# Moving the load targets of a decode kernel from 128 bytes behind a multiple of 512 in SBUF to the multiple itself

## The chip, the cores and the metric

The kernel runs on one core of one Trainium2 chip. The metric is the device time of one execution in microseconds (us). TensorE is called PE below, its loading of weights PEld, VectorE DVE, ScalarE ACT, GpSimd POOL and SyncE SP. SBUF is the memory on the chip in which tiles lie: 128 partitions, and within each partition a tile occupies a run of bytes that starts at the same address in all of them. DMA engines, 16 of them for a core, copy from the main memory (HBM) into these runs. A DMA is cut into packets; here a packet is the run of one partition, for example 32768 bytes.

## What is computed

One decoding step for two sequences: normalised input, attention over the last 4096 entries of a cache with 8 key and value heads, and beside it a dense layer with the Mish activation. The results are added to the input.

```python
def _A_ref(x, k_cache, v_cache, wq, wo):          # x: (2, 1, 448); caches: (2, 8, 32768, 256), bf16
    W = 4096
    q = (x @ wq).reshape(2, 1, 16, 256).transpose(0, 2, 1, 3)
    k = jnp.repeat(k_cache[:, :, Sk - W:, :], 2, axis=1)
    v = jnp.repeat(v_cache[:, :, Sk - W:, :], 2, axis=1)
    scores = jnp.einsum("bhqd,bhkd->bhqk", q, k) * (256 ** -0.5)
    p = softmax(scores)
    o = jnp.einsum("bhqk,bhkd->bhqd", p, v)
    return o.transpose(0, 2, 1, 3).reshape(2, 1, 4096) @ wo      # wo: (4096, 448)

def _B_ref(x, w1, b1, w2):                         # w1: (448, 1792), w2: (1792, 448)
    h = x @ w1 + b1
    return (h * jnp.tanh(softplus(h))) @ w2

xn = layernorm(A_x)
out = A_x + _A_ref(xn, ...) + _B_ref(xn, ...)
```

All of the 4096 keys and values of 16 heads (2 sequences by 8 heads) are read once: 2 x 16 x 4096 x 256 x 2 bytes = 67.1 MB, and some 10 MB of weights.

## The kernel before

Tiles come out of pools. A pool takes its bytes in SBUF in the order in which pools are opened, right behind the pool before it:

```python
    k_pool = ctx.enter_context(tc.tile_pool(name="kk", bufs=2))     # 2 x 32768 bytes per partition
    v_pool = ctx.enter_context(tc.tile_pool(name="vv", bufs=3))     # 3 x 16384
    kt_pool = ctx.enter_context(tc.tile_pool(name="kt", bufs=1))    # 2 x 32768
    wo_pool = ctx.enter_context(tc.tile_pool(name="wo", bufs=2))    # 2 x 7168
    p_pool = ctx.enter_context(tc.tile_pool(name="pp", bufs=1))
    consts = ctx.enter_context(tc.tile_pool(name="consts", bufs=1))
    small = ctx.enter_context(tc.tile_pool(name="small", bufs=2))
```

In front of the first pool lie 16384 bytes that the framework keeps and four constants of its own in 128 bytes. So the first tile of keys starts at 16512 = 32 x 512 + 128.

The loads are all issued by SP, in one queue:

```python
    def load_k(u, r):                 # 4 MB: 128 packets of 32768 bytes
        t = k_pool.tile([P, RK * KE], BF16, tag="k", name="k")
        src = kview[u][:, s0:, :].rearrange("j (c t) d -> c j (t d)", c=C)
        nc.sync.dma_start(out=t[:], in_=src[:, :, r * RK * KE : (r + 1) * RK * KE])

    def load_v(u, g, lo=0, hi=T):     # 2 MB: 128 packets of 16384 bytes
        ...
        nc.sync.dma_start(
            out=t[:, lo * Dh : hi * Dh], in_=src[g, :, :, lo * Dh : hi * Dh]
        )
    # ... load_wo: rows of 7168 bytes, for the last round of 1792; wq: 16384 and 12288; w1: 12544

    w2_parts = ((0, 0, NI), (1, 0, 4), (1, 4, 6), (1, 6, NI))      # NI = 7

    def load_w2(part):                # into a tile of the key pool, in four pieces
        if part == 0:
            state["w2"] = k_pool.tile([P, RK * KE], BF16, tag="k", name="w2")
        k, lo, hi = w2_parts[part]
        w2_in = B_w2.flatten().rearrange("(k p e) -> k p e", k=2, p=P)
        at = k * NI * D               # D = 448, two bytes each
        nc.sync.dma_start(
            out=state["w2"][:, at + lo * D : at + hi * D],
            in_=w2_in[k, :, lo * D : hi * D],
        )
```

The work runs in four rounds u; each round's keys are turned by DVE, scored by PE, and its values weighed by PE:

```python
    for u in range(U - 1):
        load_k(u + 1, 0); load_v(u, 0); load_v(u, 1)
        load_k(u + 1, 1); load_v(u, 2); load_v(u, 3)
        load_wo(u)
        turns(u + 1, 0)               # DVE: kt <- k, 128x4096 fp32 each
        values(u, 0); values(u, 1)    # PE: pv += p' v
        scores(u + 1, 0)              # PE: sc <- kt, qd; ACT: exp; DVE: p <- ex
        ...
    # last round: values, then the output projection and the second dense product
    for part in range(len(w2_parts)):
        dense_out(part)               # PE: acc += act' w2
    ...
    nc.sync.dma_start(out=out.flatten_outer_dims(), in_=res[:])
```

Of the kernel before, what the change touches and what calls it, by code (L numbers as in the profile page):

```python
# [11 lines left out]
BF16 = mybir.dt.bfloat16  # L12
# [5 lines left out]
def kernel(  # L18
# [14 lines left out]
    P = 128  # L33
# [5 lines left out]
    Bsz, Sq, D = A_x.shape  # L39
# [20 lines left out]
    NI = F2 // P  # L60
# [4 lines left out]

    ctx.enter_context(tc.manual_schedule())

    k_pool = ctx.enter_context(tc.tile_pool(name="kk", bufs=2))
    v_pool = ctx.enter_context(tc.tile_pool(name="vv", bufs=3))
    kt_pool = ctx.enter_context(tc.tile_pool(name="kt", bufs=1))  # L70
# [119 lines left out]
    for x in range(2):  # L190
        for w in range(4):
            at = 32 * w + (2 * (w % 2) + x) * NQ
# [52 lines left out]
    def add_rows(lhsT, rows, stop=False):  # L245
        for g in range(G):
            nc.tensor.matmul(  # L247
                acc[32 * g : 32 * g + Bsz, :],
                lhsT=lhsT,
                rhs=rows[:, g * DG : (g + 1) * DG],  # L250
                start=False,
                stop=stop,
                skip_group_check=True,
            )
# [257 lines left out]
    def mish():  # L512
# [20 lines left out]
        nc.vector.tensor_tensor(out=t_sb[:], in0=t_sb[:], in1=den[:], op=ALU.mult)  # L533
        nc.vector.tensor_tensor(out=act_bf[:], in0=h_sb[:], in1=t_sb[:], op=ALU.mult)

    w2_parts = ((0, 0, NI), (1, 0, 4), (1, 4, 6), (1, 6, NI))

    def load_w2(part):
        if part == 0:
            state["w2"] = k_pool.tile([P, RK * KE], BF16, tag="k", name="w2")  # L540
        k, lo, hi = w2_parts[part]
        w2_in = B_w2.flatten().rearrange("(k p e) -> k p e", k=2, p=P)
        at = k * NI * D
        nc.sync.dma_start(
            out=state["w2"][:, at + lo * D : at + hi * D],
            in_=w2_in[k, :, lo * D : hi * D],
        )

    def dense_out(part):
        k, lo, hi = w2_parts[part]  # L550
        for i in range(lo, hi):
            at = (k * NI + i) * D
            add_rows(
                act_bf[:, i, k, :], state["w2"][:, at : at + D], stop=(k == 1 and i == NI - 1)
            )
# [39 lines left out]
    for part in range(len(w2_parts)):  # L595
        load_w2(part)
# [12 lines left out]
    for part in range(len(w2_parts)):  # L609
        dense_out(part)  # L610
# [40 lines left out]
```

## Time and profile before

| | before |
|---|---|
| median of 3 executions | 191.78 us (191.65 to 191.96) |
| span of the profiled execution | 189.5 us |
| busy: PE, DVE, ACT | 93.9, 89.2, 12.3 us |
| read from HBM | 77.67 MB, 410 GB/s over the span |
| key load, 4096 KB, issue to landing | 30.3 us, median of 8 |
| value load, 2048 KB, issue to landing | 27.3 us, median of 15 |

The span is the time from the first to the last instruction in the trace. The busy times of engines run beside each other and don't add up to it. "Issue to landing" includes the time that a load stands in the queue behind older loads. In the row of 40 slices each digit is the busy share of a fortieth of the span, in tenths, 9 standing for 90% and more. The chain of work that ended last is followed backwards from the last instruction, each step to what released it.

### The profile page before, as it was taken

What the parts mean: (1) busy time and instruction counts of PE and PEld (TensorE: products, weight loads), DVE (VectorE), ACT (ScalarE), POOL (GpSimd) and SP (SyncE); (2) the same over time, 40 slices, a digit from 0 to 9 for tenths busy, and PEclk for the clock granted to TensorE, in tenths of its full rate; (3) what the DMA queues carried; (4) which work ended last, traced back from release to release, by engine and by line L of the source; (5) the groups of instructions that cost most, each with busy time, mean ns of one, the idle gap of its engine ahead of it and who ended that gap; (6) DMA issues with size and microseconds to landing.
All of it is one profiled execution on the core that took longest, in us unless ns stands there. A gap on an engine that the chain in (4) does not pass through costs nothing.

```text
span 189.5 us, 1989 instructions
## 1 busy us (share of the span) xinstructions
PE 93.9 (50%) x873; PEld 38.0 (20%) x873; DVE 89.2 (47%) x81; ACT 12.3 (7%) x23; POOL 4.0 (2%) x16
## 2 busy tenths in 40 slices
PE   0301545565139103869248033868475044969673
PEld 0100121521012001423112011413121011513361
DVE  6629643974980097017930394029900691040001
ACT  3000031001000100110001000110001001010201
POOL 8000000000000000000000000000000000000000
PEclk9999999755555855576855755555557655555975
DMA  6999999999999999999999999999999999999990
GB/s 222 443 388 425 468 408 408 456 439 401 425 495 422 387 410 436 432 429 432 429 456 429 398 429 465 423 398 418 432 456 432 398 420 431 432 406 430 404 377 28
DMA packets 5871, 77.78 MB, mean 410 GB/s; under 512 B 868, under 2 KB 1640, under 8 KB 2408
## 3 DMA queue, kind: packets, MB, share of 16 engines
q1 hardware_dynamic: 5588, 77.66, 96.7%
q8 instruction: 6, 0.10, 0.2%
q10 hardware_dynamic: 276, 0.01, 0.1%
q14 instruction: 1, 0.01, 0.0%
HBM read 77.67 MB, written 0.00 MB: 410 GB/s over the span
## 4 chain that ended last, share of the span: by engine, by line
DMA 81%; PE 9%; DVE 3%; issue 3%; SPq 2%; ACT 1%; DVEq 0%
DMA v<-in_A_v_cache_dram 59%; DMA k<-in_A_k_cache_dram 15%; DMA w<-in_B_w_dram 7%; PE pv L390 5%; DVE kt L267 2%; PE sc L345 2%; PE o L410 1%; PE acc L247 1%; PE dn L368 1%; SPq L103 1%; SPq L132 1%; SPq L95 1%; DVE p L356 0%; ACT ex L353 0%; ACT vs L404 0%
## 5 line engine op out<-in xcount | busy, mean ns | idle before, releaser
L267 DVE STREAM_TRANSPOSE kt<-k 128x4096 f32<-128x4096 f32 x16 | 70.1, 4417 | 41.0 <-DMA k<-in_A_k_cache_dram 41.0
L390 PE MATMUL pv<-v,p 128*32 128x512 bf16 x240 | 26.2, 583 | 53.7 <-DMA v<-in_A_v_cache_dram 53.7
L345 PE MATMUL sc<-kt,qd 128*32 128x512 bf16 x256 | 28.2, 614 | 3.2 <-DVE kt L267 1.8
L390 PEld LDWEIGHTS <-p 128*32 128x32 bf16 x240 | 8.5, 123 | 71.1 <-issue 64.6
L437 DVE TENSOR_TENSOR oT<-o,rec 128x16 bf16<-128x16 f32 x4 | 0.7, 174 | 29.5 <-PE o L410 16.6
L345 PEld LDWEIGHTS <-qd 128*32 128x32 bf16 x256 | 8.6, 134 | 19.6 <-issue 17.7
L356 DVE STREAM_TRANSPOSE p<-ex 128x512 bf16<-128x512 bf16 x8 | 5.2, 690 | 15.4 <-ACT ex L353 15.4
L472 PE MATMUL early<-wo,ox 128*2 128x448 bf16 x24 | 9.4, 570 | 0.8 <-ACT ox L462 0.8
L353 ACT ACTIVATE ex<-sc 128x512 bf16<-128x512 f32 x8 | 4.8, 597 | 76.5 <-PE sc L345 76.5
L289 PE MATMUL q_ps<-wq,xs 128*32 128x512 bf16 x28 | 3.4, 625 | 11.9 <-DMA wq<-in_A_wq_dram 11.9
L410 PE MATMUL o<-sel,vs 128*128 128x8 f32 x32 | 6.7, 339 | 2.8 <-ACT vs L404 2.8
L410 PEld LDWEIGHTS o<-sel,vs 128*128 128x128 f32 x32 | 6.4, 293 | 6.0 <-ACT vs L404 6.0
L368 PE MATMUL dn<-p,ones 128*128 128x512 bf16 x8 | 4.3, 540 | 6.0 <-DVE p L356 6.0
L404 ACT COPY vs<-pv 128x512 f32<-128x512 f32 x4 | 2.3, 586 | 47.2 <-PE pv L390 47.2
L502 PE MATMUL h_ps<-xs,w 128*128 128x4 bf16 x49 | 2.8, 193 | 4.3 <-DMA w<-in_B_w_dram 4.3
L334 PE MATMUL sc<-mneg,ident 128*128 128x512 bf16 x8 | 4.8, 595 | 0.0
L210 PE MATMUL xr_ps<-ident,xrows 2*128 2x2 bf16 x7 | 1.0, 181 | 6.6 <-DVE xrows L209 6.6
L376 DVE TENSOR_REDUCE rec<-dn 128x8 f32<-128x512 f32 x4 | 2.8, 692 | 2.5 <-PE dn L368 2.5
L289 PEld LDWEIGHTS <-xs 128*32 128x32 bf16 x28 | 1.0, 126 | 13.9 <-issue 13.9
L502 PEld LDWEIGHTS <-w 128*128 128x128 bf16 x49 | 2.7, 152 | 5.2 <-DMA w<-in_B_w_dram 5.2
L472 PEld LDWEIGHTS <-ox 128*2 128x2 bf16 x24 | 2.5, 115 | 5.5 <-issue 4.4
L453 PEld LDWEIGHTS <-hot 128*64 128x64 bf16 x48 | 2.0, 142 | 2.6 <-issue 2.6
(62 smaller groups left out, 37.7 us busy)
## 6 DMA issues: line engine op xcount, KB each, us to landing
k<-in_A_k_cache_dram SPq DMA_DIRECT2D x8, 4096.0 KB, 30.3
v<-in_A_v_cache_dram SPq DMA_DIRECT2D x15, 2048.0 KB, 27.3
wo<-in_A_wo_dram SPq DMA_DIRECT2D x3, 896.0 KB, 24.0
wq<-in_A_wq_dram SPq DMA_DIRECT2D x1, 2048.0 KB, 16.8
w<-in_B_w_dram SPq DMA_DIRECT2D x1, 1568.0 KB, 32.1
wq<-in_A_wq_dram SPq DMA_DIRECT2D x1, 1536.0 KB, 19.8
v<-in_A_v_cache_dram SPq DMA_DIRECT2D x1, 1536.0 KB, 10.0
wo<-in_A_wo_dram SPq DMA_DIRECT2D x2, 448.0 KB, 15.5
```

What stands on the lines that cost most here:

```text
L267: nc.vector.transpose(out=kt[i][:, :, :, r, :], in_=t[:, r * KE : (r + 1) * KE].bitcast(FP32).rearrange("p (a c j) -> p a c j", c=P // (R ...
L289: nc.tensor.matmul(q_ps[32 * u : 32 * (u + 1), :], lhsT=xs[:, s, :], rhs=wq_t[s][:, u * 512 : (u + 1) * 512], start=(s == 0), stop=(s == N ...
L334: nc.tensor.matmul(sc[:].rearrange("p t c m -> p (t c m)"), lhsT=ident[:], rhs=mneg[:].rearrange("p a j -> p (a j)"), start=True, stop=Fal ...
L345: nc.tensor.matmul(sc[32 * w : 32 * (w + 1)].rearrange("p t c m -> p t (c m)"), lhsT=qd[:, u, 2 * n + e, :, :].rearrange("p g q -> p (g q) ...
L353: nc.scalar.activation(out=ex[:, :, :, i, :], in_=sc[:], func=ACT.Exp, scale=scale)
L356: nc.vector.transpose(out=p_t[h][:].rearrange("p g t q -> p t g q"), in_=ex[:, h * TH : (h + 1) * TH].rearrange("p t c i m -> p t (c i m)" ...
L368: nc.tensor.matmul(dn[:].rearrange("p a q -> p (a q)"), lhsT=ones[:], rhs=p_t[i][:].rearrange("p g t q -> p (g t q)"), start=(i == 0), sto ...
L376: nc.vector.tensor_reduce(out=rec[:], in_=dn[:].rearrange("p a q -> p q a"), axis=AXIS.X, op=ALU.add)
L390: nc.tensor.matmul(pv[32 * w : 32 * (w + 1), :, :].rearrange("p x d -> p (x d)"), lhsT=p_t[a // 4][:, g, 4 * (a % 4) : 4 * (a % 4) + 4, :] ...
L410: nc.tensor.matmul(po[:, c, :], lhsT=sb[:, x, c::2], rhs=sel[:, x, :], start=(x == 0 and c == 0), stop=(last and x == 1), skip_group_check ...
L472: nc.tensor.matmul(early[:], lhsT=ox[:, i, :], rhs=w[:, i, :], start=False, stop=(u == U - 2 and i == 7),)
L502: nc.tensor.matmul(h_ps[:, i, :, :].rearrange("p k b -> p (k b)"), lhsT=w1_v[:, s, i, :], rhs=xs[:, s, 0 : 2 * Bsz], start=(s == 0), stop= ...
```

## The change

A tile of 192 bf16 values, 384 bytes per partition, is taken from a pool that is opened first. Nothing writes or reads it. It moves every tile behind it by 384 bytes: 128 + 384 = 512. And the second half of w2 starts 4096 values (8192 bytes) behind the first half in its tile, and not 3136 values (6272 bytes), which is no multiple of 512. The purpose is that the tiles which loads fill begin at multiples of 512 bytes.

```diff
+    lead_pool = ctx.enter_context(tc.tile_pool(name="lead", bufs=1))
+    lead_pool.tile([P, 192], BF16, name="lead")
     k_pool = ctx.enter_context(tc.tile_pool(name="kk", bufs=2))
     v_pool = ctx.enter_context(tc.tile_pool(name="vv", bufs=3))
...
+    KH = 4096
     w2_parts = ((0, 0, NI), (1, 0, 4), (1, 4, 6), (1, 6, NI))
...
-        at = k * NI * D
+        at = k * KH
         nc.sync.dma_start(
             out=state["w2"][:, at + lo * D : at + hi * D],
...
-            at = (k * NI + i) * D
+            at = k * KH + i * D
             add_rows(
                 act_bf[:, i, k, :], state["w2"][:, at : at + D], stop=(k == 1 and i == NI - 1)
```

The addresses in both programs, as built, and what they leave when divided by 512:

| tile | before | rest | after | rest |
|---|---|---|---|---|
| k, first and second buffer | 16512, 49280 | 128 | 16896, 49664 | 0 |
| v (also wq, w1), three buffers | 82048, 98432, 114816 | 128 | 82432, 98816, 115200 | 0 |
| wo, two buffers | 196736, 203904 | 128 | 197120, 204288 | 0 |
| w2, first half | 16512 | 128 | 16896 | 0 |
| w2, second half, pieces 1, 2, 3 | 22784, 26368, 28160 | 256, 256, 0 | 25088, 28672, 30464 | 0, 0, 256 |

## The prediction

> **What bounds the kernel now.** I read the page's DMA rows first, because the time is long against the engines' work: PE is busy for 50% of the span and DVE for 47%.
>
> ```profile
> span 189.5 us, 1989 instructions
> ...
> DMA  6999999999999999999999999999999999999990
> ...
> DMA packets 5871, 77.78 MB, mean 410 GB/s; under 512 B 868, under 2 KB 1640, under 8 KB 2408
> ...
> q1 hardware_dynamic: 5588, 77.66, 96.7%
> ```
>
> The DMA row stands at 9 from the second slice to the last but one, and the packets of the one big queue take 96.7% of the time of 16 DMA engines. So 0.967 x 189.5 = 183.2 us of each DMA engine is packet time. Next I looked at whether the chain of work agrees.
>
> ```profile
> DMA 81%; PE 9%; DVE 3%; issue 3%; SPq 2%; ACT 1%; DVEq 0%
> ```
>
> It does: 81% of what ended last is transfer, and the PE and DVE pieces on it are places where a load's issue waited for a buffer while older loads kept the DMA engines full. The table by stretches shows that such waits leave no hole in the stream (columns: stretch, its us, busy us of PE, PEld, DVE, ACT, POOL, granted clock, DMA share, GB/s):
>
> ```profile
> 12.00:24.00 12.00, 3.37 (x28) 0.99 (x28) 8.77 (x2) 0.54 (x1) 0.00 (x0) 1.00 1.03 437
> 24.00:60.00 36.00, 18.52 (x174) 7.75 (x178) 22.96 (x22) 2.75 (x5) 0.00 (x0) 0.66 0.99 423
> 60.00:100.00 40.00, 19.61 (x160) 7.37 (x156) 19.91 (x9) 1.95 (x4) 0.00 (x0) 0.63 1.01 429
> 100.00:140.00 40.00, 21.40 (x160) 7.96 (x163) 19.78 (x9) 1.95 (x4) 0.00 (x0) 0.54 1.01 430
> 140.00:172.00 32.00, 18.08 (x148) 6.63 (x140) 11.14 (x7) 1.82 (x4) 0.00 (x0) 0.55 1.00 421
> ```
>
> The DMA share is 1.0 in each, at 421 to 437 GB/s. Last, the end of the timeline:
>
> ```profile
> 185.49 0.83 PE L247 MATMUL acc<-w,act_bf 128*2 128x112 bf16 x17 [0.25 <-DMA w<-in_B_w_dram]
> ...
> 187.53 0.33 SPq L620 DMA_DIRECT2D out_dram<-res  x1
> ```
>
> The last weights land just before 185.5 us and what follows is about 4 us of closing work. So the time is: 2.2 us until the first packet starts, 183.2 us of packets, 4.1 us after them (that makes the span, 189.5), and 191.78 - 189.5 = 2.3 us outside the span. The kernel is bound by its own load stream from end to end, and only a shorter packet can shorten it.
>
> **What the Trainium skill says.** First, "DMA: Bandwidth & Descriptors", Specifications: the ceiling of the SBUF side is 435 GB/s, 16 engines by 32 bytes by 850 MHz, which is 27.2 bytes per ns for one engine. The trace agrees: the stretches above lie at 421 to 437 GB/s.
>
> Second, the same page, "How a descriptor splits into AXI transactions": transfers are cut at multiples of 256 bytes, and a start that is no such multiple makes the first transaction begin at the boundary below, which costs beats of 32 bytes for nothing. Before the change nearly all big tiles start 128 bytes past such a boundary: 4 beats, 4 / 0.85 = 4.7 ns per packet, an estimate from this page. The trace agrees only in part, as shown below.
>
> Third, "SBUF — State Buffer", "SBUF: two separate sides": engines and DMA reach SBUF by separate ports and do not disturb each other. So I count no gain from a changed meeting of transfers and engines. The trace neither proves nor contradicts it.
>
> Fourth, the same page, "Operand start alignment": it settles what addresses are legal and says of its own runs that they timed nothing. So no page gives a speed for 128 against 512 bytes, and the number must come from this trace.
>
> **The change, part by part.** It adds no instruction and removes none; the order on every engine is as before with shifted line numbers. The lead tile is never written or read; it costs 384 bytes per partition. All tiles behind it move by 384 bytes, so their places relative to each other stay, except that the second half of w2 lies 8192 bytes behind the first and no longer 6272. Engines should run each operation as before: the DVE transposes of 4403 ns and the matmuls keep their shapes and strides. What is left is the DMA packet.
>
> So I took the packet records of the trace: size and duration of each. What a packet takes beyond its bytes / 27.2 I call its excess:
>
> - 16384 bytes need 602.4 ns. The fastest tenth took 611 ns, the median 615, the slowest tenth 619.
> - 32768 bytes need 1204.7 ns. The same three were 1213, 1218 and 1221 ns.
> - Over all sizes there is a floor of about 8.3 ns of excess, some 7 beats. For most of the kernel packets lie at the floor, 4 to 5 ns above it, or 8 to 9 ns above it.
>
> The sum per DMA engine: 77.66 MB / 16 / 27.2 = 178.5 us for the bytes. The 4994 packets of more than 500 bytes are 312 per engine, and 312 x 8.3 ns = 2.6 us of floor. Ordinary excess above the floor (packets up to 60 ns over their bytes) sums to 1.05 us. Single packets with 60 to 800 ns excess, mostly the first one of each engine, give 0.77 us, and the little semaphore packets 0.34 us. Together 178.5 + 2.6 + 1.05 + 0.77 + 0.34 = 183.2, the packet time from above. The bytes cannot shrink. An address can touch only the 1.05 us above the floor and perhaps the floor itself.
>
> Does the misplacement cause the 1.05 us? The kernel before holds its own controls:
>
> - For: the three last pieces of w2 lie at multiples of 256 already (tile at 16512, plus 6272, 9856 and 11648 bytes: 22784, 26368, 28160). Of their 384 packets 376 are at the floor. In the same last microseconds, of 123 packets of 6272 and 4096 bytes that start 128 behind a boundary, only 84 are.
> - Against: until 23 us all tiles start 128 behind, and yet all 128 packets of 16384 bytes that fall there (the first wq piece) are at the floor, and so are 126 of the 128 packets of 12288 bytes. A fixed fee of 4.7 ns per misplaced start would show there. From 23 us on only 361 of 1920 packets of 16384 bytes are at the floor.
>
> So the fee isn't fixed, and either it arises from misplacement together with something that begins at 23 us, or from that something alone and the w2 pieces were lucky in their hour. I give the first about two chances in five. The expected gain is then 0.4 x 1.05 = 0.42 us, and 191.78 - 0.42 is about 191.4 us.
>
> **The rivals.** (1) Nothing happens: the stream is at the port's rate whatever the address, and the spread of 4 to 9 ns comes from the memory that is read, whose addresses don't change. For it speaks the clean stretch until 23 us. That gives 191.8 us, with the 0.2 us by which the three runs differ.
>
> (2) The whole spread is misplacement: 191.78 - 1.05 = 190.7 us. For it speak the w2 pieces, and that the steps of 4 to 5 ns have the size of the page's 4 beats.
>
> (3) The floor goes too. The fetches of instructions, 8192 bytes each, show 307 ns at their fastest against 301.2 for the bytes, 5.8 ns excess and not 8.3. If a wholly placed packet comes down to that, 312 x 2.5 ns = 0.8 us more, 189.9 us. Against it: the packets of w2 at multiples of 256, the last of them at a multiple of 512, have the same 8.1 to 8.6 ns as misplaced ones.
>
> (4) Slower: some engine reads worse at the new address, or the moved half of w2 meets another tile. All shifts are multiples of 128 bytes, and DVE and PE have slack: half of the span idle. DVE's transposes stand on the chain with 2% of the span, so even a tenth more on each would hardly reach 0.4 us. That gives at most 192.2 us. I see nothing that speaks for it.
>
> **Range and chances.** The centre is 191.4 us. Between rival 2 with a part of rival 3 below and rival 1 with its scatter above, a range of 190.5 to 192.0 should hold it 8 times in 10. A change of 2% is 3.8 us. All that is not bytes sums to 4.8 us and most of it is floor and start, so faster by over 2% gets 0.02, slower by over 2% 0.01, and within 2% the remaining 0.97.
>
> **What the profile after would show.** If rival 2 holds, the median 16384-byte packet falls from 615 to 611 ns and the median 32768-byte one from 1218 to 1213 ns; queue q1's share times the span falls from 183.2 to about 182.2 us, and the last weights land about 1 us earlier. If rival 1 holds, these stay within 1 ns and 0.3 us. If rival 3 holds, the fastest tenth of 16384-byte packets falls below 611 ns. DVE's 4403 ns per transpose and the engines' busy sums should be equal within a per cent in all cases. I would be wrong if DMA shares below 0.98 appeared in the stretches above (a hole in the stream), or if packets gained more than their whole excess, which would mean that 27.2 bytes per ns is not the limit I take it for.

## The result, and the profile after

The changed kernel takes 190.7 us (median of 4, 190.38 to 190.9) against 191.85 us for the kernel before on the same chip (median of 4). The ratio is 0.994 with a 95% interval from 0.9921 to 0.9958: between 0.8 and 1.5 us are gone, about 0.6%. That lies in the stated range and within 2%.

The page of the changed kernel, the lines that answer to those shown of before:

```profile
span 188.2 us, 1989 instructions
...
DMA  6999999999999999999999999999998999999990
...
DMA packets 5871, 77.78 MB, mean 413 GB/s; under 512 B 868, under 2 KB 1640, under 8 KB 2408
...
q1 hardware_dynamic: 5588, 77.66, 96.8%
...
DMA 80%; PE 10%; DVE 3%; issue 3%; SPq 2%; ACT 1%; DVEq 0%
```

The same packets, the same bytes and the same full row of 9s. The queue's share hardly moves, because the span shrank with it: 0.968 x 188.2 = 182.2 us of packets for each DMA engine, where 183.2 us stood before. The chain has the same owner with the same weight. A share says nothing here; share times span does.

The stretches of the changed kernel (stretch, its us, busy us of PE, PEld, DVE, ACT, POOL, granted clock, DMA share, GB/s):

```profile
24.00:60.00 36.00, 18.18 (x178) 7.86 (x182) 22.97 (x22) 2.63 (x4) 0.00 (x0) 0.68 0.99 425
60.00:100.00 40.00, 21.27 (x160) 7.74 (x156) 19.78 (x9) 1.95 (x4) 0.00 (x0) 0.54 1.01 434
100.00:140.00 40.00, 21.19 (x160) 7.75 (x152) 19.78 (x9) 1.95 (x4) 0.00 (x0) 0.54 1.01 434
```

There is no hole before or after: the DMA share is 1.0 in both. (A packet counts whole in the stretch in which it starts, so a short stretch can show a share of 1.03.) But 425, 434 and 434 GB/s pass where 423, 429 and 430 passed. The engines' work is what it was, as DVE's costliest group shows, first before and then after, with means of 4417 and 4414 ns:

```profile
L267 DVE STREAM_TRANSPOSE kt<-k 128x4096 f32<-128x4096 f32 x16 | 70.1, 4417 | 41.0 <-DMA k<-in_A_k_cache_dram 41.0
...
L269 DVE STREAM_TRANSPOSE kt<-k 128x4096 f32<-128x4096 f32 x16 | 70.0, 4414 | 39.9 <-DMA k<-in_A_k_cache_dram 39.9
```

At the end of the timeline everything is 1.3 us earlier, and lengths differ by 0.05 us at most (PE was at 185.49 us when it took the last weights, the output was issued at 187.53):

```profile
184.22 0.78 PE L249 MATMUL acc<-w,act_bf 128*2 128x112 bf16 x17 [0.26 <-DMA w<-in_B_w_dram]
...
186.25 0.33 SPq L623 DMA_DIRECT2D out_dram<-res  x1
```

The packet records show where the time came from. "At the floor" means at most 9.5 ns over bytes / 27.2; the excess above the floor is taken from packets up to 60 ns over their bytes, as in the prediction.

| per DMA engine, us | before | after |
|---|---|---|
| bytes | 178.46 | 178.46 |
| floor, 312 packets x 8.3 ns | 2.59 | 2.59 |
| ordinary excess above the floor | 1.05 | 0.06 |
| single packets over 60 ns | 0.77 | 0.80 |
| semaphore packets | 0.34 | 0.34 |
| all packets of the queue | 183.18 | 182.22 |
| median packet of 16384 and 32768 bytes, ns | 615, 1218 | 611, 1213 |
| packets over 500 bytes at the floor | 2016 of 4994 | 4943 of 4994 |

One term moves: the spread above the floor all but goes, 0.99 us of 1.05. That is most of the 1.15 us between the medians, and nearly all of what the prediction's second rival said would go. The semaphore packets are those of 4 bytes between the loads.

### The profile page after: what moved, and what is told of

The parts are those of the page before. It is cut to its first block, busy times and chain, and to the rows that moved or that the text cites. A ratio compares the mean times of both kernels' runs of the same rounds, so it can differ in the third digit from the quotient of the medians.

```text
span 188.2 us, 1989 instructions
## 1 busy us (share of the span) xinstructions
PE 92.1 (49%) x873; PEld 37.6 (20%) x873; DVE 89.1 (47%) x81; ACT 12.3 (7%) x23; POOL 4.0 (2%) x16
## 4 chain that ended last, share of the span: by engine, by line
DMA 80%; PE 10%; DVE 3%; issue 3%; SPq 2%; ACT 1%; DVEq 0%
DMA v<-in_A_v_cache_dram 59%; DMA k<-in_A_k_cache_dram 15%; DMA w<-in_B_w_dram 6%; PE pv L392 5%; DVE kt L269 2%; PE sc L347 2%; PE o L412 1%; PE acc L249 1%; PE dn L370 1%; SPq L134 1%; SPq L97 1%; DVE p L358 0%; SPq L105 0%; ACT ex L355 0%; ACT vs L406 0%
## 5 line engine op out<-in xcount | busy, mean ns | idle before, releaser
L269 DVE STREAM_TRANSPOSE kt<-k 128x4096 f32<-128x4096 f32 x16 | 70.0, 4414 | 39.9 <-DMA k<-in_A_k_cache_dram 39.9
L392 PE MATMUL pv<-v,p 128*32 128x512 bf16 x240 | 26.8, 593 | 54.1 <-DMA v<-in_A_v_cache_dram 54.1
L347 PE MATMUL sc<-kt,qd 128*32 128x512 bf16 x256 | 27.3, 599 | 3.2 <-DVE kt L269 1.9
L474 PE MATMUL early<-wo,ox 128*2 128x448 bf16 x24 | 8.0, 500 | 0.8 <-ACT ox L464 0.8
```

What stands on the lines that cost most here:

```text
L269: nc.vector.transpose(out=kt[i][:, :, :, r, :], in_=t[:, r * KE : (r + 1) * KE].bitcast(FP32).rearrange("p (a c j) -> p a c j", c=P // (R ...
L347: nc.tensor.matmul(sc[32 * w : 32 * (w + 1)].rearrange("p t c m -> p t (c m)"), lhsT=qd[:, u, 2 * n + e, :, :].rearrange("p g q -> p (g q) ...
L392: nc.tensor.matmul(pv[32 * w : 32 * (w + 1), :, :].rearrange("p x d -> p (x d)"), lhsT=p_t[a // 4][:, g, 4 * (a % 4) : 4 * (a % 4) + 4, :] ...
L474: nc.tensor.matmul(early[:], lhsT=ox[:, i, :], rhs=w[:, i, :], start=False, stop=(u == U - 2 and i == 7),)
```

## The experiments

My theory after the result: a packet pays a few ns when it starts off a multiple of 256 bytes in SBUF, and none of this comes from the engines. Rivals: 512 bytes are what count; the lead tile or the moved tiles of the engines are what counts; the engines' work in SBUF takes part. A further question stood from the prediction: why do misplaced packets pay nothing in the first 23 us?

**Which part of the change.** The lead tile alone, with w2 as it was:

```diff
+    lead_pool = ctx.enter_context(tc.tile_pool(name="lead", bufs=1))
+    lead_pool.tile([P, 192], BF16, name="lead")
```

> The lead tile of 384 bytes alone; the second half of w2 stays 6272 bytes behind the first, so its three pieces now start 128, 128 and 384 bytes behind a multiple of 512. If the start address of a packet is what counts: all packets but those 384 at the floor of 8 to 9 ns over their bytes, excess above the floor 0.05 to 0.15 us per DMA engine against 1.05 before, time about 190.8 us. If the part of w2 were what counts: 191.8 us.

Measured: 190.59 us, ratio 0.9938 (0.9918 to 0.9957); excess above the floor 0.06 us. The whole gain is here. One part of the expectation failed: the 384 packets of w2 that start off a multiple of 256 also lie at the floor, every one.

The other part alone:

```diff
+    KH = 4096
-        at = k * NI * D
+        at = k * KH
-            at = (k * NI + i) * D
+            at = k * KH + i * D
```

> No lead tile; only the second half of w2 moved to 8192 bytes behind the first, which here takes its pieces from 256, 256 and 0 bytes behind a multiple of 512 to 128, 128 and 384. If the start address counts: nothing gained, 191.8 to 191.9 us, 615 ns for the median packet of 16384 bytes, and some of the 384 packets of w2 that were at the floor before leave it. If the distance of the two halves of w2 matters by itself: below 191.3 us.

Measured: 191.88 us, ratio 1.0003 (0.9994 to 1.0012); excess 1.05 us. Without the lead tile this edit moves three well-placed pieces to bad places: of the 384 packets, 376 were at the floor before and about 330 are now. It brings nothing to the time, and in the full change nothing either: 190.59 us without it, 190.7 with it.

**256 or 512 bytes, and is it the address?** Both runs change one number of the changed kernel:

```diff
-    lead_pool.tile([P, 192], BF16, name="lead")
+    lead_pool.tile([P, 64], BF16, name="lead")      # rest256;  128 for rest384
```

> A lead tile of 128 bytes in place of 384: tiles start at multiples of 256 that are not multiples of 512. If the step that counts is 256 bytes: as the changed kernel, 190.7 us, median packet of 16384 bytes 611 ns, excess above the floor under 0.1 us per engine. If 512 bytes are needed, as the change has it: 191.3 to 191.9 us with medians of 613 to 615 ns.

> A lead tile of 256 bytes: tiles start 384 bytes behind a multiple of 512, 128 behind one of 256, so that everything is moved and a lead tile is there but the rest by 256 is that of before. If the start address counts: as before, 191.8 us, median 615 ns, excess above the floor about 1.05 us per engine. If merely moving the tiles of the engines (constants, scores, x) or having the pool brought the gain: 190.7 us.

Measured: rest256 190.85 us, ratio 0.9947 (0.9929 to 0.9965), excess 0.06 us; rest384 191.87 us, ratio 1.0001 (0.9993 to 1.001), excess 1.05 us. The span and the queue's line of each, first at a multiple of 256, then 128 behind one:

```profile
span 188.8 us, 1989 instructions
...
q1 hardware_dynamic: 5588, 77.66, 96.5%
```

```profile
span 189.8 us, 1989 instructions
...
q1 hardware_dynamic: 5588, 77.66, 96.4%
```

0.965 x 188.8 = 182.2 and 0.964 x 189.8 = 183.0 us. So 256 bytes are enough, 512 aren't needed, and neither the pool nor the move of the other tiles does anything: rest384 moved them too.

**How the fee grows with the rest.** Again only the size of the lead tile:

```diff
-    lead_pool.tile([P, 192], BF16, name="lead")
+    lead_pool.tile([P, 224], BF16, name="lead")     # rest64;  32 for rest192, 208 for rest32
```

> A lead tile of 448 bytes: tiles start 64 bytes behind a multiple of 256. If each packet pays for the bytes between the boundary below and its start (2 beats of 32 bytes, 2.4 ns, a second step at 4.7 ns): excess above the floor about half of before, 0.5 us per engine, 191.2 us. If any start off a multiple of 256 pays the same: 1.05 us and 191.8 us. If multiples of 64 bytes were enough: 190.7 us.

> A lead tile of 64 bytes: tiles start 192 bytes behind a multiple of 256. If each packet pays for the bytes between the boundary below and its start (6 beats, 7 ns): about 1.5 times the excess of before, 1.6 us per engine, 192.4 us. If what is paid is the distance to the next boundary (2 beats): 0.5 us, 191.2 us. If any start off a multiple of 256 pays the same: 1.05 us, 191.8 us.

> A lead tile of 416 bytes: tiles start 32 bytes behind a multiple of 512 and of 256. If the fee goes by the bytes since the boundary (1 beat): excess above the floor about 0.25 us per engine, 190.9 to 191.0 us. If any start off a multiple of 256 pays the same: 1.05 us, 191.8 us. If starts that are no multiple of 64 bytes are worse still: over 1.5 us, over 192.3 us.

| bytes behind a multiple of 256 | us | ratio to before | excess, us per engine | commonest steps of 16384-byte packets, ns over their bytes |
|---|---|---|---|---|
| 0 (rest256) | 190.85 | 0.9947 (0.9929 to 0.9965) | 0.06 | 9 |
| 128 (before) | | 1 | 1.05 | 9, 13, 17 |
| 128 (rest384) | 191.87 | 1.0001 (0.9993 to 1.001) | 1.05 | 9, 13, 17 |
| 64 (rest64) | 191.94 | 1.0003 (0.9995 to 1.0012) | 1.07 | 11, 18 |
| 192 (rest192) | 192.12 | 1.0017 (1.001 to 1.0024) | 1.15 | 11, 18 |
| 32 (rest32) | 192.21 | 1.0025 (1.0016 to 1.0033) | 1.29 | 12, 19 |

A fee by the bytes since the boundary falls: 32 bytes cost most and 192 hardly more than 64. Closest is that any start off a multiple of 256 pays about the same, with rest32 dearer by a quarter; that a start off a multiple of 64 would be worse was one of the answers set down for it, but with over 1.5 us. 64 and 192 bytes have the same steps, so the distance to the nearest boundary, not the direction, seems to set them; that is read off two runs only.

**Engines, or the stream by itself?** This run and the next three were executed once each, and it is their packet records that are read. First, the free time at the start, in the kernel before with its first load cut:

```diff
-        nc.sync.dma_start(out=t[:], in_=src[:, :, r * RK * KE : (r + 1) * RK * KE])
+        n = 4 if (u, r) == (0, 0) else 1
+        e = RK * KE // n
+        for i in range(n):
+            nc.sync.dma_start(
+                out=t[:, i * e : (i + 1) * e],
+                in_=src[:, :, r * RK * KE + i * e : r * RK * KE + (i + 1) * e],
+            )
```

> The kernel before, its tiles misplaced as they were, with the first load of keys (4 MB) cut into four DMAs of 128 packets of 8192 bytes each. It asks why misplaced packets stay at the floor until 24 us. If the fee begins after a number of packets (about 28 for each DMA engine in the kernel before), that number is reached some 24 packets earlier and the spread begins before 14 us. If it begins with SP's next issues of loads at 22 us, which wait for the first transposes, it begins at 23 to 26 us as before.

Measured: the spread begins between 19.3 and 20 us (from 20.0 to 20.6 us 12 of 20 packets are off the floor), after some 45 packets for each DMA engine. Both answers fall: a fixed count would have come long before, and the 23 us of the other answer is missed too.

Then the stream with nothing beside it. The kernel leaves out all that reads the loads and writes its input as its output:

```diff
-    turns(0, 0)
-    project()
-    scores(0, 0)
...                       # all turns, scores, weigh, values, gather, relay, mix, dense, and res from acc: left out
+    nc.vector.tensor_copy(out=res[:], in_=x_bf[:])
```

> The loads of the kernel before, in their order and at their misplaced addresses (128 behind a multiple of 256), with nothing that reads them: projection, transposes, scores, values, both products and the dense layer are left out, and the input is written as the output. SP again issues the sixth load as soon as a buffer is free, here at about 13 us, when the first keys have landed. If the fee needs SP's issues during the stream: packets leave the floor from 13 to 16 us on, and the excess above the floor is about 1 us per DMA engine. If it needs engines that work in SBUF: all packets stay at the floor, under 0.15 us per DMA engine.

Measured: excess 1.07 us, as in the full kernel, with a span of 185.6 us in which no engine works after the preparation. Its stretches, columns as above:

```profile
4.00:24.00 20.00, 1.45 (x8) 0.77 (x8) 3.92 (x24) 0.00 (x0) 0.62 (x3) 1.00 1.03 438
24.00:60.00 36.00, 0.00 (x0) 0.00 (x0) 0.00 (x0) 0.00 (x0) 0.00 (x0) 1.00 0.99 423
60.00:100.00 40.00, 0.00 (x0) 0.00 (x0) 0.00 (x0) 0.00 (x0) 0.00 (x0) 1.00 1.00 429
100.00:140.00 40.00, 0.00 (x0) 0.00 (x0) 0.00 (x0) 0.00 (x0) 0.00 (x0) 1.00 1.01 431
```

423, 429 and 431 GB/s with all engines at 0.00: the rate of the misplaced stream in the full kernel (423, 429, 430), while well-placed tiles under full work reach 425, 434 and 434. So engines play no part, and the rival that they do falls. The other expectation fails as well: SP issues at 13.2 and 18.2 us, yet all but a few packets stay at the floor until 24 us.

The same with PE at work:

```diff
+    busy = ps_sc.tile([P, 512], FP32, tag="sc", name="busy")
+    for i in range(480):
+        nc.tensor.matmul(busy[:], lhsT=ident[:], rhs=mneg[:].rearrange("p a j -> p (a j)"), ...)
```

> As loads_alone, with 480 matmuls of 512 columns on two constant tiles from about 8 us on, which read nothing that a load fills. If TensorE's reading of SBUF brings the fee: packets leave the floor with the first matmul and come back to it after the last one. If SP's issues bring it: as loads_alone, from 13 us on to the end. If neither: at the floor throughout, under 0.15 us per DMA engine.

Measured: excess 1.03 us. Packets begin to leave the floor at 25 us, 17 us after the first matmul, and don't come back when PE ends at 114 us. PE is out too.

**Does the free time come back?** With room for both placements, a third run of loads alone chooses per round:

```diff
+    off = {"at": 64}                                   # elements: 128 bytes
-        return v_pool.tile([P, KE], BF16, tag="v", name=name)
+        t = v_pool.tile([P, KE + 128], BF16, tag="v", name=name)
+        return t[:, off["at"] : off["at"] + KE]
+        off["at"] = 0 if u == 1 else 64                # in the loop over rounds; keys likewise
```

The wo weights and the first half of w2 are well placed throughout.

> Loads alone again (all computing left out, the input written as the output), with room for both placements: keys, values and weights of the first part (to about 58 us) start 128 bytes behind a multiple of 256, those of the second part (about 58 to 97 us) at multiples of 256, those of the third part (from about 97 us; the wo weights and the first half of w2 excepted) again 128 behind. The fee should be absent in the second part in any case, and be back at the floor with its first packets. For the third part: if misplaced packets pay only after the 16 engines have run misplaced for some 25 packets each (an order at the start of the stream that wears off), the third part begins at the floor and leaves it 10 to 25 us later. If it is only the beginning of the whole stream that is free of the fee, packets pay from 97 us on at once, 3 to 4 ns above the floor in the mean.

The expected times are those of issue; by landing the second part begins near 75 us and the third at 116.6 us. What the packets did (large ones):

| part | us | at the floor | mean excess over the bytes, ns |
|---|---|---|---|
| misplaced | 34.5 to 72 | 174 of 734 | 12.2 |
| well placed | 75 to 112 | 704 of 704 | 8.5 |
| misplaced again, first | 116 to 146 | 523 of 523 | 8.3 to 8.5 |
| then | 148 to 154 | 22 of 160 | 12.0 |

All large packets of the well-placed part are at the floor; of the 128 packets of the wo load that leads into it (from 73.5 us), 12 of the first 0.4 us still pay. Misplaced packets after this part ride free for 30 us, 32 packets of each DMA engine, and then pay. After one short well-placed load (wo, 8 packets each, until 157.7 us) they ride free again, but only until 160 us. After the last such load, wo with 32 short packets for each engine (until 170.0 us), 383 of 384 misplaced packets are at the floor, to 179.8 us. So in this run the free time isn't bound to the start of the stream: it follows each of the three well-placed stretches. This would also explain lead_only: its misplaced pieces of w2 are 24 packets per engine behind a well-placed stream, and the kernel is over before they pay.

The run also goes against the theory in its plain form. Of the 128 packets of w2's first half (179.4 to 181.4 us), which start at multiples of 256, 32 pay, most of them 5 to 7 ns above the floor, and they come behind those 24 misplaced packets per engine that paid nothing. So a packet's own start doesn't settle what it pays. What the runs show is a rule for the stream: where its targets start at multiples of 256 the spread stays away, and misplaced ones bring it up after a while.

**What the floor itself costs.** The changed kernel with each load of keys in two DMAs:

```diff
-        nc.sync.dma_start(out=t[:], in_=src[:, :, r * RK * KE : (r + 1) * RK * KE])
+        for i in range(RK):
+            at = (r * RK + i) * KE
+            nc.sync.dma_start(out=t[:, i * KE : (i + 1) * KE], in_=src[:, :, at : at + KE])
```

> The changed kernel (well-placed tiles) with each load of keys cut into two DMAs, 128 packets of 16384 bytes each in place of 128 of 32768: 1024 more packets, 64 for each DMA engine. If every packet costs its floor of 8.3 ns whatever its place: 64 x 8.3 = 0.53 us more packet time per DMA engine than the changed kernel's 182.2 us, so 182.7 to 182.8 us, and a time of about 191.2 us. If the floor is hidden behind the packet before it: packet time and time as in the changed kernel, 182.2 and 190.7 us. A third outcome is an earlier start of the first transposes, which could not shorten the end, since the stream sets it.

Measured: 191.16 us, ratio 0.997 (0.9961 to 0.9979) to the kernel before; 0.46 us above the changed kernel by the medians. Packet time per DMA engine is 182.92 us, 0.70 more than in the changed kernel: 0.53 from the 64 floors, 0.07 from more semaphore packets, 0.06 from more excess just after the start and 0.05 from single slow packets. The floor is paid per packet, not hidden. Two lines of its page:

```profile
span 188.9 us, 1994 instructions
...
q1 hardware_dynamic: 6740, 77.66, 96.9%
```

## Why the prediction was right, point by point

- *The load stream alone bounds the kernel.* Right. 0.96 us less packet time is 1.15 us less by the medians and 1.3 us less span in the profiled execution; these agree within the 0.5 us by which the four runs differ.
- *The budget: 178.5 + 2.6 + 1.05 + 0.77 + 0.34 us.* Right, and it named the one term that could move. That term fell to 0.06, all others stayed within 0.03 us.
- *The engines are untouched, rival 4 has nothing for it.* Right: transposes 4414 against 4417 ns. The Trainium skill's "SBUF — State Buffer", "SBUF: two separate sides", says that engines and DMA don't disturb each other there; loads_alone agrees, with 1.07 us of excess without the engines against 1.05 us with them.
- *Does the misplacement cause the 1.05 us? Two chances in five.* Here the weighing went off: 191.4 us stood for 0.4 of the term, and it was nearly the whole of it, as in rival 2 (190.7 us; packets of 611 and 1213 ns; 182.2 us of packets). The range held because it took in both answers; the answer that was given three chances in five was the wrong one. The evidence "for" (the last w2 pieces) was sound. The evidence "against", the clean 23 us at the start, was read as pointing to memory. loads_three_parts shows how else it can be read: misplaced packets also ride free for a while behind a well-placed stretch, so a clean stretch doesn't speak against misplacement. Why the very start is free no run shows.
- *4 beats per misplaced start, after "DMA: Bandwidth & Descriptors", "How a descriptor splits into AXI transactions".* The section puts the waste in bytes that are fetched, hence in reading, and the prediction carried it over to tiles that are written. That the boundary lies at 256 bytes holds for these writes too, by rest256 against rest384. The fee by the bytes since the boundary is not: rests of 32, 64, 128 and 192 bytes cost 1.29, 1.07, 1.05 and 1.15 us. The mean fee here was 1.05 us / 312 = 3.4 ns a packet, not 4.7.
- *Rival 3, a lower floor.* Wrong: well-placed packets have the same 8 to 9 ns, and keys_in_halves shows them to be paid for each packet.
- *Rival 1, nothing happens.* Wrong: the interval of the ratio ends at 0.9958.

What stays open is what it is in the stream that well-placed packets restore and misplaced ones lose after a while. That the 16 DMA engines keep a relation to each other which misplaced packets upset would fit, but no run shows it; the records don't say which DMA engine carried a packet, and I haven't tried the stream on fewer of them.

## What to carry to other kernels

Where a kernel is one full DMA stream, take the packet records, subtract bytes at the port's rate, and count what is left per packet: the sum of floors shrinks with fewer, longer packets, and here the spread above them went when the load targets started at multiples of 256 bytes. Both are small in this kernel, mostly of packets of 16 to 32 KB (1.4% and 0.5% of the time). The floor is much the same for packets of 896 bytes (8.1 ns) and of 32768 (8.3 ns), so its share should grow as packets shrink; no run here timed that. An unused tile at the head of SBUF was enough here, 128 bytes per partition in rest256, and a part of the stream that looks clean isn't proof that its placement is good.

## What the runs showed of the hardware that I had not expected

- In loads_three_parts misplaced packets pay nothing for 30 us after a well-placed stretch of about 40 us, for about 3 us after one of 8 packets per DMA engine, and for 10 us after one of 32 short ones. And well-placed packets can pay, 32 of 128 at 179.4 to 181.4 us.
- A start 32 bytes behind a multiple of 256 is the dearest measured, 1.29 us of excess per DMA engine (rest32).
- Packets of 475 to 560 ns excess follow most fetches of instructions: in loads_and_pe these start at 27.2, 55.4, 83.0 and 110.5 us and such packets at 28.3, 56.4, 84.0 and 111.5 us. In loads_alone, with 158 instructions in the profile and no such fetch, there is none after 6 us. They are half of a microsecond on one DMA engine each. The rule has exceptions: in the kernel before, five of six fetches have such a packet behind them, and one of 671 ns at 70.3 us has no fetch before it.
